# A mask by one product in place of two selects, and a new order of the opening stages, in a sliding-window attention and FFN kernel

## The chip, the cores and the metric

The kernel runs on one core of a Trainium2 chip. The metric is the device time of one execution in microseconds (us). The core has five engines with queues of their own: TensorE (PE; its weight loads are listed apart as PEld), VectorE (DVE), ScalarE (ACT), GpSimd (POOL) and SyncE (SP, which here only issues transfers). They run side by side, and wait for each other by semaphores. Within one queue the order written in the program holds: an instruction that waits holds back all behind it.

## The reference

Eight batches of eight heads with 576 positions of width 64 go through causal attention with a window of 64 positions. The heads are then laid side by side into 4608 tokens of width 512, which go through a multiplicative feed-forward network (FFN):

```python
scores = scale * np.matmul(q, k.transpose(0, 1, 3, 2))
rel = pos[:, None] - pos[None, :]
mask = (rel >= 0) & (rel < window)
attn = softmax(np.where(mask, scores, -1e9))      # over keys
x = np.matmul(attn, v)                            # then (batch*seq, heads*64)
a = x @ w1
b = x @ w2
h = a * b @ w3
out = h @ w_out
```

All inputs and the output are float32.

## The kernel before

**Attention.** The kernel works in float16 with float32 sums. For a batch, K and Q are loaded with the sequence folded onto 128 partitions, cast to float16 (`cast_qk`, L226; for batch 0 in thirds, `cast_third`, L229), transposed by PE into PSUM and copied out into `kT` and `qT` (`transposes`, L262 and L266). A batch is then six steps d: three segments of the sequence times two halves of the head pairs, so that batch 0 is d = 0 to 5 and batch 1 is d = 6 to 11. `scores(d)` multiplies K by Q into the PSUM tile `s_ps`, of which there is one; ACT takes the exponential into `pt` (L300), of which there are six; and POOL sets to zero what lies outside the window. It does so with pairs of `affine_select` (L308 and L310): one pair over 1024 elements a partition in the second and third segment, and two pairs, over 512 and 256, in the first. `values(d)` multiplies V, stored with columns of ones that give the sums, by `pt` into `o_ps` or `s_ps`; ACT makes the reciprocal of the sum by a logarithm and an exponential, and DVE writes the product into `xT`, a ring that holds four batches.

V of batch 0 is loaded in rows and brought into place by transposes (`transposes(0, "v", ...)`, then `keys_of_v`, L273 and L275). For later batches `load_v` (L241) writes V straight into `v16s`, with five DMAs issued by POOL, and `copy_v` (L245, L247) has DVE copy the halves of blocks that overlap.

**The fold.** As nothing is between w3 and w_out, the kernel computes their product once. `fold_t(fc)` transposes a block row of w3 (L492, L493), and `fold_mm(fc, half)` multiplies it by one half of w_out into `wc_sb` (L501, L503). w3 comes in four pieces (`load_w3(n)`, each for two fc), w_out in two halves.

**The FFN.** A group g is 512 tokens. `ffn_ab(g, fc)` for eight fc makes a and b on PE (L432), ACT copies a (L437), DVE multiplies (L438); `ffn_o(g, t)` for four t multiplies by the folded weights (L450), DVE copies (L452), and SP stores (`store`, L459).

**PSUM.** PE writes into tiles of four pools: `tp` (one), `s_ps` (one), `o_ps` (one) and `f_ps` (three). `three()` gives banks of the first three, in a stated order, to the three thirds of a transpose. `keep_busy(n)` issues n matmuls into `tp` whose result nobody reads.

**Order.** It is written out by hand: no scheduler moves anything. The order of calls in the program is the order on every queue. First come the loads of K and Q of batch 0 (SP and ACT queues) and a row of loads on POOL's queue, then the scores of batch 0 mixed with the fold, then the values of batch 0 with the rest of the fold, then FFN group 0 mixed with the scores and values of batch 1. Afterwards a loop goes through the FFN groups 1 to 8, and after each piece `tick(u)` adds the attention steps that are due by a count written in the code; that part isn't touched, apart from the mask inside `scores`. Loads of K and Q from batch 2 on go through SP and are held back by a small memset of the buffer that they write (`gate` in `load_qk`, L208); their casts are made by POOL.

Of the kernel before, what the change touches and what calls it, by code (L numbers as in the profile page):

```python
# [9 lines left out]
FP16 = mybir.dt.float16  # L10
I32 = mybir.dt.int32
ALU = mybir.AluOpType
# [3 lines left out]
P = 128  # L16
# [128 lines left out]
def kernel(  # L145
# [67 lines left out]
    def load_rows(b, which):  # L213

        t = sb.tile([P, 2, TI * D], FP16, name="rows", bufs=3)
        for hh in range(2):
            nc.gpsimd.dma_start(out=t[:, hh], in_=big_rows(which, b, hh))
        raws[which, b] = t
# [6 lines left out]
    def cast_qk(b, which, hh, cp):  # L225
        cp(t16_of(b, which)[:, :, hh * D:hh * D + D], raws[which, b][:, hh].rearrange("p (i d) -> p i d", d=D))  # L226
# [25 lines left out]
    def transposes(b, which, *cs, into=None, cps=None):  # L252

        t16 = t16s[which, b]
        if cs[0] == 0:
            turned[which, b] = sb.tile([P, NJ, S], FP16, name=which + "T", bufs=1 if which == "v" else 2)
        dst = turned[which, b]
        if into is None:
            into = [ps_t.tile([P, 6, P], FP16, name="tp")]
        for c, tp in zip(cs, into):  # L260
            for i in range(6):
                nc.tensor.transpose(tp[:, i, :], t16[:, 6 * c + i, :], ident16)  # L262
        if cps is None:
            cps = [dve_cp if which == "k" or c != 1 else act_cp for c in cs]
        for c, tp, cp in zip(cs, into, cps):
            cp(dst.rearrange("q j (p i) -> q j p i", i=TI)[:, :, :, 6 * c:6 * c + 6],  # L266
               tp.rearrange("q i (p j) -> q j p i", p=TP))

    def keys_of_v(b, js, into, cps):
# [4 lines left out]
        for j, tp, cp in zip(js, into, cps):  # L274
            cp(v16s[b % 2][:, :, j].rearrange("p c (a e) -> p c a e", a=2)[:, :, :, 0:D],  # L275
               tp.rearrange("p c (a e) -> p c a e", a=2))


    MASKS = [[(0, 1, 128, 0, 0), (128, 1, 64, 64, 0)]] + 2 * [[(0, 2, 128, 64, -64)]]
    probs, lns = {}, {}  # L280

    def scores(d):

        b, r = divmod(d, 6)
        si, jp = divmod(r, 2)
        kT, qT = turned["k", b], turned["q", b]
        seg = SEGS[si]
        w = sum(blk[2] for blk in seg)
        s_ps = ps_s.tile([P, 2, 2, 256], FP32, name="s_ps")
        for jj in range(2):  # L290
            j = 2 * jp + jj
            c0 = 0
            for (k0, q0, n, _) in seg:
                for a in range(2):
                    half = slice(a * D, a * D + D)
                    nc.tensor.matmul(s_ps[:, a, jj, c0:c0 + n], kT[half, j, k0:k0 + P], qT[half, j, q0:q0 + n],  # L296
                                     start=True, stop=True, skip_group_check=True)
                c0 += n
        pt = sb.tile([P, 2, 2, 256], FP16, name="pt", bufs=6)
        nc.scalar.activation(pt[:, :, :, 0:w], s_ps[:, :, :, 0:w], AF.Exp, bias=-SHIFT, scale=scale)  # L300

        rows = pt.rearrange("k a j n -> k (a j) n")
        for (lo, nb, n, off, step) in MASKS[si]:
            sl = rows[:, :, lo:lo + nb * n]
            pat = [[0, 4], [step, nb], [1, n]]
            if nb == 1:
                pat = [[0, 4], [1, n]]
            nc.gpsimd.affine_select(out=sl, in_=sl, pattern=pat, compare_op=ALU.is_ge,  # L308
                                    fill=0.0, base=off, channel_multiplier=-1)
            nc.gpsimd.affine_select(out=sl, in_=sl, pattern=[[-s, m] for s, m in pat], compare_op=ALU.is_ge,  # L310
                                    fill=0.0, base=63 - off, channel_multiplier=1)
        probs[d] = pt

    def values(d, pool=None):
# [154 lines left out]
    def load_w12(i, half):  # L469
        cols = slice(half * 512, half * 512 + 512)  # L470
        nc.gpsimd.dma_start(out=(w1_sb, w2_sb)[i][:, :, cols],
                            in_=(moe_w1, moe_w2)[i][:, cols].rearrange("(c p) n -> p c n", p=P))

    def load_wo(half):
        cols = slice(half * 256, half * 256 + 256)
        nc.gpsimd.dma_start(out=wo16[:, :, cols], in_=moe_w_out[:, cols].rearrange("(e p) m -> p e m", p=P))

    def load_w3(n):
        fc = 2 * n
        dst = w3a[:, 2 * fc:2 * fc + 4, :].rearrange("p (f a) n -> p f (a n)", f=2) if n < 2 else \  # L480
            xT[:, fc - 4:fc - 2, 2 * S:2 * S + DF]
        nc.gpsimd.dma_start(out=dst, in_=moe_w3[fc * P:fc * P + 2 * P].rearrange("(f p) n -> p f n", p=P))
# [12 lines left out]
    def fold_mm(fc, half, cp, nf=1):  # L495

        cols = slice(half * 256, half * 256 + 256)
        o_ps = ps_f.tile([P, 2, 256], FP32, name="f_ps")
        for f in range(nf):
            for ec in range(8):  # L500
                nc.tensor.matmul(o_ps[:, f], turned_w3(fc + f)[:, ec, :], wo16[:, ec, cols],  # L501
                                 start=(ec == 0), stop=(ec == 7), skip_group_check=True)
        cp(wc_sb[:, fc:fc + nf, cols], o_ps[:, 0:nf])  # L503
# [19 lines left out]
    def keep_busy(n):  # L523

        d = ps_t.tile([P, P], FP32, name="tp")
        for _ in range(n):
            nc.tensor.matmul(d, ident16, ident16, start=True, stop=True)
# [7 lines left out]
    def ones_of(i):  # L535
        nc.gpsimd.memset(v16s[i].rearrange("p c j (a e) -> p (c j a) e", a=2)[:, :, D:2 * D], 1.0)

    ones_of(0)
    load_w3(0)
    load_wo(0)  # L540
    load_rows(0, "v")
    for n in range(1, 4):
        load_w3(n)
    load_wo(1)
    ones_of(1)

    def bank(pool, name):

        t = pool.tile([P, 2, 1024] if name != "f_ps" else [P, 1, 1024], FP16, name=name)
        return t[:, 0, 0:768].rearrange("p (i n) -> p i n", i=6)  # L550

    def tp_bank():
        return ps_t.tile([P, 6, P], FP16, name="tp")

    def three():
        return [bank(ps_v, "o_ps"), tp_bank(), bank(ps_s, "s_ps")]

    keep_busy(75)
    for c in range(3):
# [11 lines left out]
    fold_t(1)  # L571
    for i in range(2):
        load_w12(i, 0)
    scores(2)
    fold_mm(0, 0, dve_cp)
    scores(3)
    load_rows(1, "k")
    fold_mm(1, 0, dve_cp)
    for hh in range(2):
        cast_qk(0, "v", hh, dve_cp)  # L580
    scores(4)
    keep_busy(10)
    transposes(0, "v", 0, 1, 2, into=[bank(ps_v, "o_ps"), tp_bank(), bank(ps_f, "f_ps")], cps=[dve_cp, act_cp, act_cp])
    fold_t(2)
    fold_t(3)
    scores(5)
    load_rows(1, "q")
    for i in range(2):
        load_w12(i, 1)
    load_v(1, 0, 2, 3)  # L590
    keys_of_v(0, [0, 1, 2], [bank(ps_v, "o_ps"), tp_bank(), bank(ps_f, "f_ps")], [act_cp, dve_cp, dve_cp])
    fold_mm(2, 0, act_cp)
    keys_of_v(0, [3], [tp_bank()], [dve_cp])
    fold_t(4)
    fold_mm(3, 0, act_cp)
    fold_t(5)
    values(0)
    fold_mm(4, 0, act_cp)
    fold_t(6)
    values(1, ps_s)  # L600
    fold_mm(5, 0, act_cp)
    fold_t(7)
    values(2)
    fold_mm(6, 0, dve_cp)
    values(3, ps_s)
    fold_mm(7, 0, dve_cp)
    values(4)
    fold_mm(0, 1, dve_cp, 2)
    values(5, ps_s)
    fold_mm(2, 1, dve_cp, 2)  # L610
    fold_mm(4, 1, dve_cp, 2)
    load_v(1, 4, 5)
    load_qk(2, "k", nc.gpsimd.memset)
    load_qk(2, "q")
    fold_mm(6, 1, dve_cp, 2)
    cast_qk(1, "k", 0, dve_cp)
    cast_qk(1, "k", 1, act_cp)
    for n in range(3):
        keep_sums(n)


    ffn_ab(0, 0)
    transposes(1, "k", 0, 1, 2, into=three(), cps=[dve_cp, act_cp, dve_cp])
    cast_qk(1, "q", 0, dve_cp)
    cast_qk(1, "q", 1, act_cp)
    for hh in range(2):
        cast_qk(2, "k", hh, pool_cp)
    ffn_ab(0, 1)
    transposes(1, "q", 0, 1, 2, into=three(), cps=[dve_cp, act_cp, dve_cp])
    ffn_ab(0, 2)  # L630
    scores(6)
    ffn_ab(0, 3)
    scores(7)
    copy_v(1, 1)
    for hh in range(2):
        cast_qk(2, "q", hh, pool_cp)
    ffn_ab(0, 4)
    scores(8)
    copy_v(1, 4)
    load_v(2, 0, 2, 3)  # L640
    ffn_ab(0, 5)
    scores(9)
    load_qk(3, "k")
    steps = [lambda fc=fc: ffn_ab(0, fc) for fc in range(6, 8)] + [lambda t=t: ffn_o(0, t) for t in range(4)]
    for d in range(6, 12):
        values(d, ps_s if d in (9, 11) else None)
        if d < 8:
            scores(d + 4)
        steps.pop(0)()
        store()  # L650
        if d == 6:
            load_v(2, 4, 5)
        if d > 8:
            transposes(2, "k", d - 9)
    for hh in range(2):
        cast_qk(3, "k", hh, pool_cp)
    transposes(2, "q", 0, 1, 2, into=three())
    load_qk(3, "q")
    copy_v(2, 1)
    copy_v(2, 4)  # L660
# [68 lines left out]
```

## Time and profile before

| | |
|---|---|
| median of 14 runs | 293.43 us (291.67 to 297.34) |
| profiled execution | 293.63 us |
| its span in the profile | 291.8 us |
| granted TensorE clock | 0.997 of full speed |
| PE busy | 275.7 us in 2429 matmuls |
| POOL busy | 180.0 us |
| POOL selects, L308 and L310 | 52.5 and 52.1 us, 64 of each |
| moved by DMA | 37.68 MB |

A line of the groups by shape reads: line, engine, operation, output and input, shapes, count; then busy time and the mean duration in ns; then the idle time of the engine just before these instructions and what ended it. In the list of waits each row has the waiting engine and line, what it waited for, the total in us, how many times, and the longest. In the table by stretch of time each engine has its busy time and its number of instructions. In the timeline and in the chain a row begins with the start in us and the duration.

### The profile page before, as it was taken

To read this page: it belongs to the slowest core of one execution; us is meant where nothing else is said; L and a number is where in the kernel's file an instruction comes from. 1 tells how busy PE (TensorE), PEld (TensorE's weight loads), DVE (VectorE), ACT (ScalarE), POOL (GpSimd) and SP (SyncE) were. 2 spreads that over 40 slices of the span, in tenths; PEclk is the share of its full clock that TensorE was granted. 3 is DMA by queue.
4 is the path that set the end of the run, shared out by engine and by line. 5 is a ranking of instruction groups with operands and counts; after the bars stand their busy time and mean duration, and the time that the engine had idled before them with its cause. 6 is when DMAs were issued, how large, how long until landed. Compare 5 with 4: busy or idle time off the path is not lost.

```text
span 291.8 us, 6248 instructions
## 1 busy us (share of the span) xinstructions
PE 275.7 (94%) x2429; PEld 161.9 (55%) x2429; DVE 184.4 (63%) x280; ACT 167.7 (57%) x277; POOL 180.0 (62%) x215
## 2 busy tenths in 40 slices
PE   7589998989899999999999999999999999999991
PEld 7568885445554555555555886455555545444441
DVE  0946558535868477778687866687767655464541
ACT  2565644674267646866777556478567765732300
POOL 8779933599479938695789473786595444402200
PEclk9999999999999999999999999999999999999998
DMA  6999999929797838294749550940193011002012
GB/s 243 247 210 204 209 211 372 169 16 93 149 388 107 80 124 317 14 105 140 299 31 125 187 211 0 193 37 2 37 172 22 2 73 73 2 36 110 2 61 89
DMA packets 48449, 37.68 MB, mean 129 GB/s; under 512 B 34160, under 2 KB 38512, under 8 KB 48416
## 3 DMA queue, kind: packets, MB, share of 16 engines
q0 software_dynamic: 38960, 11.14, 36.8%
q1 hardware_dynamic: 9024, 24.79, 23.2%
q10 hardware_dynamic: 432, 1.31, 1.3%
q8 instruction: 20, 0.33, 0.5%
q14 instruction: 13, 0.11, 0.1%
HBM read 38.80 MB, written 9.44 MB: 165 GB/s over the span
## 4 chain that ended last, share of the span: by engine, by line
PE 80%; POOL 7%; DVE 6%; ACT 2%; DMA 2%; issue 1%; DVEq 0%; POOLq 0%; SPq 0%; ACTq 0%
PE f_ps L432 38%; PE f_ps L450 20%; PE o_ps L354 5%; PE tp L262 5%; PE f_ps L501 5%; PE s_ps L296 4%; POOL pt L310 2%; POOL pt L308 2%; DMA stage<-in_k_dram 2%; DVE kT L266 1%; POOL v L241 1%; DVE k L229 1%; ACT pt L300 1%; PE f_ps L492 1%; PE s_ps L338 1%
## 5 line engine op out<-in xcount | busy, mean ns | idle before, releaser
L432 PE MATMUL f_ps<-xT,w_sb 128*128 128x512 f16 (+1 forms) x640 | 134.4, 358 | 0.0
L308 POOL TENSOR_SCALAR_AFFINE_SELECT pt<-pt 128x512 f16<-128x512 f16 (+1 forms) x64 | 52.5, 820 | 62.3 <-ACT pt L300 62.3
L432 PEld LDWEIGHTS <-w_sb 128*128 128x128 f16 x640 | 59.7, 98 | 50.3 <-issue 0.3
L450 PE MATMUL f_ps<-wc_sb,ab 128*128 128x512 f16 (+1 forms) x296 | 67.0, 373 | 0.1
L438 DVE TENSOR_TENSOR ab<-f_ps,a_sb 128x512 f16<-128x512 f32 x72 | 49.7, 691 | 22.1 <-PE f_ps L432 18.6
L300 ACT ACTIVATE pt<-s_ps 128x1024 f16<-128x1024 f32 (+1 forms) x48 | 45.7, 952 | 21.5 <-PE s_ps L296 19.1
L437 ACT COPY a_sb<-f_ps 128x512 f32<-128x512 f32 x72 | 41.7, 580 | 27.8 <-PE f_ps L432 26.8
L310 POOL TENSOR_SCALAR_AFFINE_SELECT pt<-pt 128x512 f16<-128x512 f16 (+1 forms) x64 | 52.1, 813 | 4.5
L363 DVE TENSOR_TENSOR xT<-o_ps,r 64x384 f16<-64x384 f32 x36 | 19.8, 549 | 38.7 <-ACT r L362 38.7
L450 PEld LDWEIGHTS <-ab 128*128 128x128 f16 x296 | 27.4, 98 | 27.9 <-issue 0.3
L360 ACT ACTIVATE ln_s<-o_ps 64x384 f32<-64x384 f32 x36 | 17.5, 487 | 32.6 <-PE o_ps L354 32.6
L452 DVE COPY t2k<-f_ps 128x512 f32<-128x512 f32 (+1 forms) x36 | 24.5, 682 | 11.8 <-PE f_ps L450 11.4
L241 POOL DMA_DIRECT2D v<-in_v_dram x35 | 29.7, 862 | 0.0
L354 PEld LDWEIGHTS <-v 128*128 128x128 f16 x288 | 18.1, 98 | 8.7 <-ACT pt L300 0.8
L296 PEld LDWEIGHTS <-kT 64*128 64x128 f16 x384 | 10.9, 94 | 18.6 <-issue 16.8
L354 PE MATMUL o_ps<-pt,v 128*128 128x128 f16 (+1 forms) x288 | 20.7, 215 | 0.4 <-DVE xT L364 0.4
L226 POOL CAST k<-stage 128x1152 f16<-128x1152 f32 x12 | 13.7, 1149 | 11.0 <-PE s_ps L262 8.1
L364 DVE TENSOR_TENSOR xT<-o_ps,r 64x384 f16<-64x384 f32 x36 | 20.2, 561 | 0.5
L296 PE MATMUL s_ps<-qT,kT 64*128 64x128 f16 (+1 forms) x384 | 18.2, 214 | 1.8 <-ACT pt L300 1.4
L362 ACT ACTIVATE r<-ln_s 128x384 f32<-128x384 f32 x36 | 18.8, 522 | 1.2
L361 ACT ACTIVATE ln_s<-o_ps 64x384 f32<-64x384 f32 x36 | 17.4, 482 | 0.4
L266 DVE COPY kT<-tp 128x768 f16<-128x768 f16 x18 | 17.1, 950 | 0.0
(88 smaller groups left out, 238.5 us busy)
## 6 DMA issues: line engine op xcount, KB each, us to landing
out_dram<-t2k SPq DMA_DIRECT2D x35, 256.0 KB
stage<-in_k_dram SPq DMA_DIRECT2D x13, 576.0 KB
stage<-in_q_dram SPq DMA_DIRECT2D x13, 576.0 KB
v<-in_v_dram POOLq DMA_DIRECT2D x28, 128.0 KB, 4.4
w_sb<-in_moe_w_dram POOLq DMA_DIRECT2D x4, 512.0 KB, 10.9
ab<-in_moe_w_dram POOLq DMA_DIRECT2D x2, 512.0 KB, 10.7
ab<-in_moe_w_out_dram POOLq DMA_DIRECT2D x2, 512.0 KB, 14.4
xT<-in_moe_w_dram POOLq DMA_DIRECT2D x2, 512.0 KB, 16.4
```

What stands on the lines that cost most here:

```text
L241: nc.gpsimd.dma_start(out=vh[lo:P, c], in_=v[b, :, s0:s0 + P - lo, :].rearrange("h s d -> s h d"))
L296: nc.tensor.matmul(s_ps[:, a, jj, c0:c0 + n], kT[half, j, k0:k0 + P], qT[half, j, q0:q0 + n], start=True, stop=True, skip_group_check=True)
L300: nc.scalar.activation(pt[:, :, :, 0:w], s_ps[:, :, :, 0:w], AF.Exp, bias=-SHIFT, scale=scale)
L308: nc.gpsimd.affine_select(out=sl, in_=sl, pattern=pat, compare_op=ALU.is_ge, fill=0.0, base=off, channel_multiplier=-1)
L310: nc.gpsimd.affine_select(out=sl, in_=sl, pattern=[[-s, m] for s, m in pat], compare_op=ALU.is_ge, fill=0.0, base=63 - off, channel_multip ...
L354: nc.tensor.matmul(o_ps[:, jj, o0:o0 + n], v16[:, si * 2 + bi, j0 + jj, a * D:a * D + P], pt[:, a, jj, c0:c0 + n], start=first, stop=(bi = ...
L364: nc.vector.tensor_tensor(xs[D:P], o_ps[D:P, :, 192:384], r[D:P], ALU.mult)
L432: nc.tensor.matmul(d[:, f * n + c0:f * n + c1], w[:, dc, (fc + f) * P:(fc + f + 1) * P], xT[:, dc, xc:xc + c1 - c0], start=first, stop=(dc ...
L437: act_cp(a_sb[:, 0:nf * n], a_ps[:, 0:nf * n])
L438: nc.vector.tensor_tensor(ab[:, fc:fc + nf, lo:hi], b_ps[:, 0:nf * n].rearrange("p (f n) -> p f n", f=nf), a_sb[:, 0:nf * n].rearrange("p ...
L450: nc.tensor.matmul(o_ps[:, 0:c1 - c0], ab[:, fc, t * P:t * P + P], wc_sb[:, fc, c0:c1], start=(fc == 0), stop=(fc == 7))
L452: cp(o_sb[:, c0:c1], o_ps[:, 0:c1 - c0])
```

## The change

The change has two parts.

The mask: `make_mask` builds once, on POOL, a float16 tile of 128 x 256 ones and zeros with a memset and two selects. In `scores`, POOL then multiplies `pt` by that tile, repeated over the four (half, pair) planes: one product of 1024 elements in the second and third segment, and two, of 512 and 256, in the first.

The order: the memset of ones for the second V buffer and the second piece of w3 stand ahead of the load of V of batch 0. Products of the fold come ahead of the next scores, and four of them instead of two ahead of V's transposes; ten filler matmuls become six there. K and Q of batch 1 are cast two steps sooner, and K is transposed before the first FFN piece. The gate of the loads of K of batch 2 is on DVE and behind the first FFN piece. The POOL casts of K and Q of batch 2, the copies of V of batch 1 and the values of batch 1 stand later among the FFN pieces. The banks of `three()` are in another order, and who copies them out is stated anew.

```diff
+    mask = const.tile([P, 2 * P], FP16)
+    def make_mask():
+        nc.gpsimd.memset(mask, 1.0)
+        pat = [[-64, 2], [1, P]]
+        nc.gpsimd.affine_select(out=mask, in_=mask, pattern=pat, compare_op=ALU.is_ge,
+                                fill=0.0, base=64, channel_multiplier=-1)
+        nc.gpsimd.affine_select(out=mask, in_=mask, pattern=[[-s, m] for s, m in pat], compare_op=ALU.is_ge,
+                                fill=0.0, base=63 - 64, channel_multiplier=1)
...
-        for (lo, nb, n, off, step) in MASKS[si]:
...
-            nc.gpsimd.affine_select(out=sl, in_=sl, pattern=pat, compare_op=ALU.is_ge,
-                                    fill=0.0, base=off, channel_multiplier=-1)
-            nc.gpsimd.affine_select(out=sl, in_=sl, pattern=[[-s, m] for s, m in pat], compare_op=ALU.is_ge,
-                                    fill=0.0, base=63 - off, channel_multiplier=1)
+        for (lo, n, m0) in [(0, 128, 128), (128, 64, 0)] if si == 0 else [(0, 256, 0)]:
+            sl = rows[:, :, lo:lo + n]
+            nc.gpsimd.tensor_tensor(sl, sl, mask[:, m0:m0 + n].unsqueeze(1).to_broadcast([P, 4, n]), ALU.mult)
...
     ones_of(0)
+    ones_of(1)
     load_w3(0)
     load_wo(0)
+    load_w3(1)
     load_rows(0, "v")
-    for n in range(1, 4):
+    for n in range(2, 4):
         load_w3(n)
     load_wo(1)
-    ones_of(1)
+    make_mask()
...
-        return [bank(ps_v, "o_ps"), tp_bank(), bank(ps_s, "s_ps")]
+        return [bank(ps_v, "o_ps"), bank(ps_s, "s_ps"), tp_bank()]
...
+    fold_mm(0, 0, dve_cp)
     scores(2)
-    fold_mm(0, 0, dve_cp)
+    fold_mm(1, 0, dve_cp)
     scores(3)
     load_rows(1, "k")
-    fold_mm(1, 0, dve_cp)
+    fold_t(2)
+    fold_t(3)
+    scores(4)
+    fold_mm(2, 0, act_cp)
     for hh in range(2):
         cast_qk(0, "v", hh, dve_cp)
-    scores(4)
-    keep_busy(10)
-    transposes(0, "v", 0, 1, 2, ...)
-    fold_t(2)
-    fold_t(3)
+    fold_mm(3, 0, act_cp)
     scores(5)
...
+    keep_busy(6)
+    transposes(0, "v", 0, 1, 2, ...)
+    fold_t(4)
+    fold_t(5)
     keys_of_v(0, [0, 1, 2], ...)
...
     values(5, ps_s)
-    fold_mm(2, 1, dve_cp, 2)
-    fold_mm(4, 1, dve_cp, 2)
-    load_v(1, 4, 5)
-    load_qk(2, "k", nc.gpsimd.memset)
-    load_qk(2, "q")
-    fold_mm(6, 1, dve_cp, 2)
     cast_qk(1, "k", 0, dve_cp)
     cast_qk(1, "k", 1, act_cp)
+    load_v(1, 4, 5)
+    fold_mm(6, 1, dve_cp, 2)
+    cast_qk(1, "q", 0, dve_cp)
+    cast_qk(1, "q", 1, act_cp)
...
+    transposes(1, "k", 0, 1, 2, into=three(), cps=[act_cp, dve_cp, dve_cp])
     ffn_ab(0, 0)
-    transposes(1, "k", 0, 1, 2, into=three(), cps=[dve_cp, act_cp, dve_cp])
-    cast_qk(1, "q", 0, dve_cp)
-    cast_qk(1, "q", 1, act_cp)
-    for hh in range(2):
-        cast_qk(2, "k", hh, pool_cp)
+    load_qk(2, "k", nc.vector.memset)
+    load_qk(2, "q")
     ffn_ab(0, 1)
-    transposes(1, "q", 0, 1, 2, into=three(), cps=[dve_cp, act_cp, dve_cp])
+    transposes(1, "q", 0, 1, 2, into=three(), cps=[act_cp, dve_cp, act_cp])
     ffn_ab(0, 2)
     scores(6)
     ffn_ab(0, 3)
     scores(7)
-    copy_v(1, 1)
+    for hh in range(2):
+        cast_qk(2, "k", hh, pool_cp)
+    ffn_ab(0, 4)
+    scores(8)
     for hh in range(2):
         cast_qk(2, "q", hh, pool_cp)
-    ffn_ab(0, 4)
-    scores(8)
-    copy_v(1, 4)
     load_v(2, 0, 2, 3)
-    ffn_ab(0, 5)
-    scores(9)
     load_qk(3, "k")
-    steps = [lambda fc=fc: ffn_ab(0, fc) for fc in range(6, 8)] + [lambda t=t: ffn_o(0, t) for t in range(4)]
+    steps = [lambda fc=fc: ffn_ab(0, fc) for fc in range(5, 8)] + [lambda t=t: ffn_o(0, t) for t in range(4)]
     for d in range(6, 12):
-        values(d, ps_s if d in (9, 11) else None)
-        if d < 8:
-            scores(d + 4)
         steps.pop(0)()
         store()
+        if d in (6, 8):
+            copy_v(1, {6: 1, 8: 4}[d])
+        if d < 9:
+            scores(d + 3)
+        values(d, ps_s if d in (9, 11) else None)
         if d == 6:
             load_v(2, 4, 5)
         if d > 8:
             transposes(2, "k", d - 9)
     for hh in range(2):
         cast_qk(3, "k", hh, pool_cp)
-    transposes(2, "q", 0, 1, 2, into=three())
+    steps.pop(0)()
+    store()
+    transposes(2, "q", 0, 1, 2, into=three(), cps=[act_cp, act_cp, dve_cp])
```

Where the diff has "...", lines that stay, or the like of which are shown, are left out: between the transposes of V and values(5), each fold piece of the second half of w3 stands one place sooner than before.

More of the change, by code (lines that the diff above doesn't have):

```diff
@@ L276, in keys_of_v @@
                tp.rearrange("p c (a e) -> p c a e", a=2))
-    MASKS = [[(0, 1, 128, 0, 0), (128, 1, 64, 64, 0)]] + 2 * [[(0, 2, 128, 64, -64)]]
     probs, lns = {}, {}
+    mask = const.tile([P, 2 * P], FP16)
[6 more added lines that the diff above has]
+                                fill=0.0, base=63 - 64, channel_multiplier=1)
     def scores(d):
@@ L302, in scores @@
         rows = pt.rearrange("k a j n -> k (a j) n")
-        for (lo, nb, n, off, step) in MASKS[si]:
[L304 to L308, printed above, removed]
-                                    fill=0.0, base=off, channel_multiplier=-1)
-            nc.gpsimd.affine_select(out=sl, in_=sl, pattern=[[-s, m] for s, m in pat], compare_op=ALU.is_ge,
-                                    fill=0.0, base=63 - off, channel_multiplier=1)
+        for (lo, n, m0) in [(0, 128, 128), (128, 64, 0)] if si == 0 else [(0, 256, 0)]:
+            sl = rows[:, :, lo:lo + n]
+            nc.gpsimd.tensor_tensor(sl, sl, mask[:, m0:m0 + n].unsqueeze(1).to_broadcast([P, 4, n]), ALU.mult)
         probs[d] = pt
@@ L573 @@
         load_w12(i, 0)
+    fold_mm(0, 0, dve_cp)
     scores(2)
-    fold_mm(0, 0, dve_cp)
+    fold_mm(1, 0, dve_cp)
     scores(3)
     load_rows(1, "k")
-    fold_mm(1, 0, dve_cp)
+    fold_t(2)
+    fold_t(3)
+    scores(4)
+    fold_mm(2, 0, act_cp)
     for hh in range(2):
         cast_qk(0, "v", hh, dve_cp)
-    scores(4)
-    keep_busy(10)
-    transposes(0, "v", 0, 1, 2, into=[bank(ps_v, "o_ps"), tp_bank(), bank(ps_f, "f_ps")], cps=[dve_cp, act_cp, act_cp])
-    fold_t(2)
-    fold_t(3)
+    fold_mm(3, 0, act_cp)
     scores(5)
@@ L590 @@
     load_v(1, 0, 2, 3)
+    keep_busy(6)
+    transposes(0, "v", 0, 1, 2, into=[bank(ps_v, "o_ps"), tp_bank(), bank(ps_f, "f_ps")], cps=[dve_cp, act_cp, act_cp])
+    fold_t(4)
+    fold_t(5)
     keys_of_v(0, [0, 1, 2], [bank(ps_v, "o_ps"), tp_bank(), bank(ps_f, "f_ps")], [act_cp, dve_cp, dve_cp])
-    fold_mm(2, 0, act_cp)
+    fold_mm(4, 0, act_cp)
     keys_of_v(0, [3], [tp_bank()], [dve_cp])
-    fold_t(4)
-    fold_mm(3, 0, act_cp)
-    fold_t(5)
+    fold_t(6)
+    fold_mm(5, 0, act_cp)
     values(0)
-    fold_mm(4, 0, act_cp)
-    fold_t(6)
+    fold_t(7)
+    fold_mm(6, 0, act_cp)
     values(1, ps_s)
-    fold_mm(5, 0, act_cp)
-    fold_t(7)
+    fold_mm(7, 0, act_cp)
     values(2)
-    fold_mm(6, 0, dve_cp)
+    fold_mm(0, 1, dve_cp, 2)
     values(3, ps_s)
-    fold_mm(7, 0, dve_cp)
+    fold_mm(2, 1, dve_cp, 2)
     values(4)
-    fold_mm(0, 1, dve_cp, 2)
+    fold_mm(4, 1, dve_cp, 2)
     values(5, ps_s)
-    fold_mm(2, 1, dve_cp, 2)
-    fold_mm(4, 1, dve_cp, 2)
-    load_v(1, 4, 5)
-    load_qk(2, "k", nc.gpsimd.memset)
-    load_qk(2, "q")
-    fold_mm(6, 1, dve_cp, 2)
     cast_qk(1, "k", 0, dve_cp)
     cast_qk(1, "k", 1, act_cp)
+    load_v(1, 4, 5)
+    fold_mm(6, 1, dve_cp, 2)
+    cast_qk(1, "q", 0, dve_cp)
+    cast_qk(1, "q", 1, act_cp)
     for n in range(3):
         keep_sums(n)
+    transposes(1, "k", 0, 1, 2, into=three(), cps=[act_cp, dve_cp, dve_cp])
     ffn_ab(0, 0)
-    transposes(1, "k", 0, 1, 2, into=three(), cps=[dve_cp, act_cp, dve_cp])
-    cast_qk(1, "q", 0, dve_cp)
-    cast_qk(1, "q", 1, act_cp)
-    for hh in range(2):
-        cast_qk(2, "k", hh, pool_cp)
+    load_qk(2, "k", nc.vector.memset)
+    load_qk(2, "q")
     ffn_ab(0, 1)
-    transposes(1, "q", 0, 1, 2, into=three(), cps=[dve_cp, act_cp, dve_cp])
+    transposes(1, "q", 0, 1, 2, into=three(), cps=[act_cp, dve_cp, act_cp])
     ffn_ab(0, 2)
```

## The prediction

> **What bounds the kernel now.** First the page's first part: TensorE is busy for 94% of the span, nothing else for more than 63%.
>
> ```profile
> PE 275.7 (94%) x2429; PEld 161.9 (55%) x2429; DVE 184.4 (63%) x280; ACT 167.7 (57%) x277; POOL 180.0 (62%) x215
> ```
>
> Next the table by stretch (length; busy time of PE, PEld, DVE, ACT, POOL; clock, DMA share, GB/s), cut where the stages change.
>
> ```profile
> 14.30:44.00 29.70, 27.81 (x397) 23.55 (x397) 16.32 (x27) 16.92 (x27) 22.43 (x30) 1.00 1.22 209
> 44.00:78.80 34.80, 31.33 (x315) 17.11 (x314) 21.68 (x32) 18.50 (x30) 23.37 (x27) 1.00 0.88 159
> 78.80:250.00 171.20, 170.82 (x1412) 94.83 (x1410) 120.84 (x188) 115.61 (x195) 116.11 (x138) 1.00 0.55 118
> ```
>
> From 78.8 to 250 us PE idles 0.4 us, so a cheaper mask gains nothing there. It idles 1.9 us in the fold stage and 3.5 us in the stage of batch 1; every reordering edit lies there or ahead. The waits of PE from 44 to 90 us name the second sum:
>
> ```profile
> PE o_ps L262 <- DVE q L226: 1.2, 1, 1.2
> PE s_ps L296 <- ACT pt L300: 1.1, 1, 1.1
> PE tp L262 <- DVE kT L266: 1.0, 1, 1.0
> PE o_ps L354 <- DVE xT L364: 0.4, 1, 0.4
> PE s_ps L338 <- POOL pt L310: 0.2, 1, 0.2
> ```
>
> In the fold stage the largest is 1.0 us, for the cast of V (L226). The chain that ended last nevertheless runs through POOL from 54 to 74 us:
>
> ```profile
> 63.08 2.60 POOL v L241 x3
> 65.68 1.13 POOL pt L308
> 74.06 0.64 PE s_ps L338 x16
> ```
>
> PE waits for it only 0.24 us: POOL and PE are tied there, and speeding up PE alone would turn into waits for POOL.
>
> [...]
>
> ```profile
> 7.27 3.13 DVE L229 CAST k<-stage 128x768 f16<-128x768 f32 x1
> 128.53 1.69 DVE L245 COPY v<-v 64x512 f16<-64x512 f16 x1
> ```
>
> The same cast took 0.59 just before, and the copy 0.29 where POOL was idle. The first got through when POOL's run of DMA issues ended at 10.0, the second between L308 and L310. So DVE gets in where POOL has a gap, and L310, waiting for L308, made one.
>
> [...] The groups by shape have:
>
> ```profile
> L308 POOL TENSOR_SCALAR_AFFINE_SELECT pt<-pt 128x1024 f16<-128x1024 f16 x32 | 35.6, 1112 | 34.5 <-ACT pt L300 34.5
> L310 POOL TENSOR_SCALAR_AFFINE_SELECT pt<-pt 128x1024 f16<-128x1024 f16 x32 | 35.2, 1099 | 2.3
> L513 POOL TENSOR_TENSOR chk<-lnsum 48x768 f32<-48x768 f32 x1 | 1.5, 1460 | 12.9 <-DMA out_dram<-t2k 12.9
> ```
>
> **Mask.** The selects took 0.42, 0.64 and 1.11 us for 256, 512 and 1024 elements: some 0.18 fixed. L513 then gives 1.28/768 = 1.67 ns an element, and the product over 1024 elements is 0.18 + 1.71 = 1.9 us against 2.21 + 0.07 gap; 512 + 256 cost 1.0 + 0.6 against 2.12 + 0.2. [...] Lower: a float16 product as fast as one select, 1.1. I take 1.9, since L513 is this operation, in another type. POOL saves 0.4 to 0.7 us a step, nearly all hidden. Building the mask (a memset and two selects of 256, about 1.2 us) fits ahead of the first exponential, which ends at 16.06.
>
> **Start, +0.4 us.** The q transposes fill o_ps, s_ps, tp rather than o_ps, tp, s_ps. The six filler matmuls behind them write tp, now emptied last (ACT, 14.82). Before, they ran from 14.31 under that copy; now their 0.34 us follow it, and scores(0) goes from 14.87 to about 15.25. The second memset of v (2.85) moves ahead of the weight loads: issues run from 6.9 to 13.1, not 4.0 to 10.0. K and Q fill the DMA engines until about 9.8, so the loads land little later. But the DVE casts of K, asked from 6.76, now meet a longer run of issues. In before, one got in at 6.9 next to an issue of V; V stands at 9.5 to 10.6 now. If the third cast gets in there it ends at 11.0 instead of 10.40, and Q's cast still ends at 13.4, because that was held by the memset until 12.98 and is now held by the last issue until 13.05. That is the value I take. Bounds: −1.0 if casts slip between issues; +2.7 if the third cast waits for 13.1.
>
> **Loads.** Landings in before: w3(0) 11.8, w_out 14.4, V 16.8 and 18.1, second w3 20.6, third 23.1: one after another, about 2.5 us for 512 KB. Swapped, the second w3 lands near 17.1 and V near 20.8. Needed: fold_t(2) at 20.0, V's casts at 21.9. Neither waits; cover 2.9 and 1.1 us.
>
> **Fold stage, −1.4 us.** Walking PE with row durations (scores 0.35, fold transposes 0.45, product 0.92, exponentials 0.81 and 1.02): fold_t(2), fold_t(3), fold_mm(2) and fold_mm(3) fill the place where PE waited 1.0 us for V's cast, and four fillers (0.2) go. Scores(3) and (4) wait 0.3 us each for the exponential before, as s_ps is single. The ACT copies of vT now stand behind exp(5), end at 26.6, and cost 0.5 us before keys_of_v. Values(0) comes at 30.25 with fold_t(7), fold_mm(6), (7) and half 1 left: 12.7 us, to 42.95, where ffn_ab(0,0) stood at 44.03. Net of the start, −1.4 (bounds −2.0 to −0.8).
>
> **Batch 1, −1.3 us.** Casts of K and Q two steps sooner: PE waits about 0.4 us for ACT's half of K (1.13, behind values(5)), but the 1.2 us for Q's cast goes. The bank order and ffn_o(0,3) placed before the q transposes remove the 1.0 us wait for tp; a full FFN step before scores(9) removes the 1.1. Scores(6) starts at 50.65 instead of 52.78.
>
> POOL now becomes the limit. From the mask of d=7 at 54.0 it has, without a pause: that mask 1.7, K cast 2.25, mask 1.9, Q cast 2.25, three V loads 2.6, mask 1.9, two V loads 1.6, masks 1.9 and 1.9, to 72.0. PE would stand for 2.4 us before values(9) and values(10). Also copy_v(1,1), moved behind ffn_ab(0,5), [...] its two copies get in about 58 to 60, so values(6) starts near 60.3 instead of 57.35; xT of values(6) and the next FFN product are queued on DVE behind them. That stall overlaps POOL's. Then ffn_ab(1,0) is at 76.9, against 78.84, start and fold included; with no copy stall 76.1. K of batch 2, gated now by a DVE memset at about 46.9 instead of POOL's at 38.95, lands about 52 and is cast at 55.7: hidden, cover 3.5 us. The later gate also leaves V of batch 1 the DMA engines: it landed at 54 to 57.5 before, and comes sooner. On SP, K and Q of batch 2 and K of batch 3 go out in one row ahead of the first store; each buffer is free, so nothing there waits. POOL's third to fifth V issue of batch 1 wait for landings of K and Q of batch 1 (about 35 to 37.5), with only the mask of d=6, at 52, behind them.
>
> **Sum.** +0.4 − 1.4 − 1.3 = −2.3 us. The profiled execution took 293.63 with span 291.8, so about 289.5 + 1.8 = 291.3; against the median 293.43, 291.1.
>
> **Rivals.** (1) *Faster still*: the product is nearer 1.1 us and casts slip between issues. POOL sheds 3 us, copies enter early, the start gains up to 1. All idle PE time is 5.4 us, so 287.9 to 289.9, say 289. [...]
> (2) *The start loses what is gained*: the K casts wait for the whole run of issues, as the 3.13 us row did. Scores(0) at about 17.2, 1.9 us later than in my sum: 293.0.
> (3) *Slower*: a single product leaves no L308–L310 gap. If copy_v is shut out through mask, Q cast and V loads, values(6) starts at 65.3. From there PE needs 16.3 us to ffn_ab(1,0): 81.6, or +2.8 us: 296.2. It decides when the second copy ends after 62.5. Against: copies at 55.8 to 58.2 got in within 0.1 us between small selects.
> (4) *The mask isn't cheaper*[...]
>
> **How the numbers follow.** Forecast 0.42 (own range 290.0 to 292.2); rivals 0.18, 0.20, 0.14, 0.06. The range 288.2 to 295.3 leaves out the deep end of (1) and most of (3). A measurement here tells about 0.5%, 1.5 us: faster 0.36 + 0.18 + 0.03 = 0.57; same 0.06 + 0.15 + 0.05 = 0.26; slower 0.17.
>
> **What would show it.** Scores(0) at 15.2 or 17; the product's mean[...]; no wait of PE for V's or Q's cast; the L245 and L247 copies near 58 to 60; values(9) or (10) waiting for POOL; ffn_ab(1,0) at about 77; then PE without idle time. A copy held past 62 us, or casts of K ending after 13, would make the prediction wrong.

## The result, and the profile after

The changed kernel takes 305.53 us (median of 10 runs, 303.58 to 307.35), against 293.16 for the kernel before in the same runs: a ratio of 1.042 [1.038, 1.045]. It is 4.2% slower, where 291.1 was predicted. The profiled execution's span is 304.8 us, 13.0 longer than the 291.8 before.

Page of the changed kernel: busy time of each engine, the granted clock in 40 slices.

```profile
PE 280.6 (92%) x2425; PEld 163.9 (54%) x2425; DVE 195.8 (64%) x277; ACT 170.3 (56%) x281; POOL 174.2 (57%) x153
...
PEclk9887799998999999999999999999999999999999
```

POOL has less to do than before (174.2 us against 180.0), as intended. But DVE is busy for 11.4 us longer with three instructions fewer, so some of its instructions became longer, and the clock is below full in the slices (7.6 us each) from 8 to 38 us and from 69 to 76. The groups by shape tell which instructions (busy time, mean in ns, then idle time before):

```profile
L312 POOL TENSOR_TENSOR pt<-pt,mask 128x1024 f16<-128x1024 f16 x32 | 68.1, 2132 | 39.3 <-ACT pt L307 39.3
...
L245 DVE COPY v<-v 64x512 f16<-64x512 f16 x14 | 18.4, 1314 | 1.1 <-DMA v<-in_v_dram 0.8
...
L226 DVE COPY k<-rows 128x1152 f16<-128x1152 f16 x3 | 9.4, 3156 | 0.0
L229 DVE CAST k<-stage 128x768 f16<-128x768 f32 x2 | 1.1, 580 | 6.8 <-DMA stage<-in_k_dram 6.8
```

Three of them in the kernel before:

```profile
L245 DVE COPY v<-v 64x512 f16<-64x512 f16 x14 | 8.7, 621 | 1.4 <-DMA v<-in_v_dram 1.1
...
L229 DVE CAST k<-stage 128x768 f16<-128x768 f32 x2 | 3.6, 1858 | 6.8 <-DMA stage<-in_k_dram 6.8
...
L226 DVE COPY k<-rows 128x1152 f16<-128x1152 f16 x3 | 2.2, 772 | 0.0
```

The product of 1024 takes 2.13 us, about as long as the pair of selects that it replaces (2.21 plus a gap of 0.07); those of 512 and 256 take 1.15 and 0.67. The copies from SBUF to SBUF on DVE changed most; those out of PSUM did not (`kT<-tp` of L266 has a mean of 950 ns before and after). L245 has a mean of 1314 ns where it had 621, and L226 (two casts of V and one of K) 3156 where it had 772; 447 ns is what an undisturbed L226 takes in this trace. L229, the cast of K at the start, went the other way, from 1858 to 580.

The waits of PE (total, times, longest, in us) show what these copies hold up. Before, the first of them was 1.0 us and the other three weren't in the list:

```profile
PE o_ps L262 <- DVE k L226: 6.7, 1, 6.7
...
PE o_ps L339 <- DVE v L247: 2.7, 1, 2.7
PE f_ps L433 <- DVE t2k L453: 2.3, 3, 1.0
PE f_ps L433 <- DVE ab L439: 2.1, 3, 1.4
```

The first is the wait for V of batch 0, in the fold stage. The timeline of that stage (start, duration, engine, line) shows both sides of it:

```profile
20.04 4.21 POOL L312 TENSOR_TENSOR pt<-pt,mask 128x1024 f16<-128x1024 f16 x2
21.39 8.94 DVE L226 COPY k<-rows 128x1152 f16<-128x1152 f16 x2
24.19 1.14 POOL L217 DMA_DIRECT2D rows<-in_k_dram  x2
25.34 4.20 POOL L312 TENSOR_TENSOR pt<-pt,mask 128x1024 f16<-128x1024 f16 x2
...
30.39 0.82 PE L262 MATMUL o_ps<-ident,k 128*128 128x128 f16 x6 [6.66 <-DVE k L226]
```

POOL runs from 20.04 without a pause: two products, two DMA issues, two products, two issues. The first cast of V starts at 21.39 and ends at 29.87, with the first of the last two issues; the second is over 0.47 later. So DVE did not wait for the product that was running alone, but through all four and the issues between them.

In the stage of batch 1 it is the second of the two copies of V that waits:

```profile
66.09 0.29 DVE L245 COPY v<-v 64x512 f16<-64x512 f16 x1
66.18 2.18 POOL L312 TENSOR_TENSOR pt<-pt,mask 128x1024 f16<-128x1024 f16 x1
66.41 2.09 DVE L247 COPY v<-v 64x512 f16<-64x512 f16 x1
68.56 0.64 PE L339 MATMUL o_ps<-pt,v 128*64 128x64 f16 x12 [2.73 <-DVE v L247]
69.13 3.03 PE L433 MATMUL f_ps<-xT,w_sb 128*128 128x512 f16 x8
```

L245 gets in behind POOL's casts of K, which ran from 63.98 to 66.2, and takes its bare 0.29; L247 is then held for the whole product. The last row shows a second cost: an FFN piece that took 1.90 us at full clock takes 3.03. The table by stretch (length; busy time of PE, PEld, DVE, ACT, POOL; clock, DMA share, GB/s) shows a low clock after both waits:

```profile
30.40:34.00 3.60, 3.60 (x35) 3.60 (x36) 1.57 (x2) 1.52 (x2) 2.59 (x4) 0.51 1.20 210
...
69.00:73.00 4.00, 4.00 (x39) 1.81 (x36) 1.25 (x2) 2.01 (x4) 4.00 (x5) 0.69 0.22 14
...
87.00:250.00 163.00, 158.49 (x1316) 88.09 (x1315) 123.04 (x175) 107.33 (x181) 105.20 (x88) 1.00 0.57 119
```

After the wait of 6.7 us the clock is half for 3.6 us, and PE does 1.8 us of work less in them; in the row behind the wait of 2.7 us it is half for about 2.5 us, 1.2 us of work less.

The last of those rows is the loop, where PE had idled 0.4 us in all from 78.8 on; now it idles 4.5 us from 87 to 250. One of its waits in the timeline:

```profile
135.60 1.16 POOL L226 CAST k<-stage 128x1152 f16<-128x1152 f32 x1
136.50 3.59 DVE L245 COPY v<-v 64x512 f16<-64x512 f16 x1
136.71 2.13 POOL L312 TENSOR_TENSOR pt<-pt,mask 128x1024 f16<-128x1024 f16 x1
138.79 1.15 POOL L226 CAST k<-stage 128x1152 f16<-128x1152 f32 x1
...
141.06 2.12 POOL L312 TENSOR_TENSOR pt<-pt,mask 128x1024 f16<-128x1024 f16 x1 [1.13 <-ACT pt L307]
...
141.88 1.45 DVE L245 COPY v<-v 64x512 f16<-64x512 f16 x1
...
144.42 1.02 PE L433 MATMUL f_ps<-xT,w_sb 128*128 128x512 f16 x4 [0.96 <-DVE t2k L453]
```

The first copy waits through a cast, a product and another cast, the next through the rest of a product. The output copies (L453) in DVE's queue behind them are late, the three tiles of f_ps stay full, and PE stands at 143.5. The loop has several such places.

Added up: scores(0) starts at 13.49 instead of 14.87, a gain of 1.4 us. The first piece of FFN group 1 starts at 86.81 instead of 78.84, a loss of 8.0. In between stand the two waits of 9.4 us and the 3.0 us of work lost to the clock behind them; that these 12.4 exceed the 8.0 leaves 4.4 us that the new order gains there, the start's 1.4 among them. (A third stretch at half clock, from 13.4 to 16.8 us, lies in between too, so this gain is after what that cost.) The rest of the span, +5.0 us, is the loop and what follows it.

### The profile page after: what moved, and what is told of

It reads as the page before. It is cut to its first block, busy times and chain, and to the rows that moved or that the text cites. A ratio compares the mean times of both kernels' runs of the same rounds, so it can differ in the third digit from the quotient of the medians.

```text
span 304.8 us, 6174 instructions
## 1 busy us (share of the span) xinstructions
PE 280.6 (92%) x2425; PEld 163.9 (54%) x2425; DVE 195.8 (64%) x277; ACT 170.3 (56%) x281; POOL 174.2 (57%) x153
## 4 chain that ended last, share of the span: by engine, by line
PE 73%; DVE 11%; issue 8%; ACT 5%; POOL 1%; DVEq 0%; POOLq 0%; ACTq 0%
PE f_ps L433 36%; PE f_ps L451 14%; PE tp L262 5%; PE o_ps L355 4%; PE s_ps L303 4%; PE f_ps L502 3%; DVE k L226 3%; PE tp L528 3%; DVE t2k L453 2%; PE f_ps L493 1%; DVE v L245 1%; DVE ab L439 1%; PE o_ps L339 1%; DVE v L247 1%; DVE xT L365 1%
## 5 line engine op out<-in xcount | busy, mean ns | idle before, releaser
L312 POOL TENSOR_TENSOR pt<-pt,mask 128x512 f16<-128x512 f16 (+1 forms) x64 | 96.6, 1522 | 90.0 <-ACT pt L307 90.0
L433 PE MATMUL f_ps<-xT,w_sb 128*128 128x512 f16 (+1 forms) x640 | 135.8, 360 | 4.4 <-DVE t2k L453 2.3
L453 DVE COPY t2k<-f_ps 128x512 f32<-128x512 f32 (+1 forms) x36 | 24.4, 681 | 11.1 <-PE f_ps L451 10.6
L245 DVE COPY v<-v 64x512 f16<-64x512 f16 x14 | 18.4, 1314 | 1.1 <-DMA v<-in_v_dram 0.8
L266 DVE COPY kT<-tp 128x768 f16<-128x768 f16 x19 | 18.0, 950 | 0.0
L226 POOL CAST k<-stage 128x1152 f16<-128x1152 f32 x12 | 13.7, 1150 | 3.2 <-issue 3.2
```

Of the source, the lines that this page charges most:

```text
L312: nc.gpsimd.tensor_tensor(sl, sl, mask[:, m0:m0 + n].unsqueeze(1).to_broadcast([P, 4, n]), ALU.mult)
L433: nc.tensor.matmul(d[:, f * n + c0:f * n + c1], w[:, dc, (fc + f) * P:(fc + f + 1) * P], xT[:, dc, xc:xc + c1 - c0], start=first, stop=(dc ...
L453: cp(o_sb[:, c0:c1], o_ps[:, 0:c1 - c0])
```

## The experiments

Four theories stand against each other. *No gap*: the single product leaves POOL's queue without a gap, and DVE's copies are shut out. *The order*: the new order costs the time, whatever the mask is made with. *Late V*: V of batch 0 lands later, since its load went behind a piece of w3. *A dear product*: what counts is POOL's own time for the mask. Unless said otherwise a diff is against the changed kernel. Where two kernels are compared, their ratios to the kernel before are subtracted and multiplied by 293 us.

### The new order with the old mask

```diff
-        for (lo, n, m0) in [(0, 128, 128), (128, 64, 0)] if si == 0 else [(0, 256, 0)]:
-            sl = rows[:, :, lo:lo + n]
-            nc.gpsimd.tensor_tensor(sl, sl, mask[:, m0:m0 + n]...)
+        for (lo, nb, n, off, step) in MASKS[si]:
...                                        # the pair of selects of the kernel before
-    make_mask()
```

> The new order kept whole, the mask made by the two selects again. Theory A (the single product leaves GpSimd without a gap, so that VectorE's copies from SBUF to SBUF[...], wait for the whole queue of GpSimd): each pair of selects has a gap, so the first cast of V takes under 3 us instead of 8.47, TensorE's 6.7 us wait for it and its half-speed clock behind it go, copies of V take under 1.8 us each, and the time is 288 to 293 us. Theory B (the new order itself costs the time, V's casts being asked for while GpSimd is busiest): the waits of 6.7 and 2.7 us stay and the time is above 299 us.

Measured: 292.0 us, ratio 0.993 [0.990, 0.996]. The order alone is a gain of 0.7%. The theory of the order falls, and the product costs 14 us here. The timeline shows the casts of V at the same place:

```profile
20.31 1.72 DVE L226 COPY k<-rows 128x1152 f16<-128x1152 f16 x2
20.47 1.24 POOL L316 TENSOR_SCALAR_AFFINE_SELECT pt<-pt 128x1024 f16<-128x1024 f16 x1
21.78 1.20 POOL L318 TENSOR_SCALAR_AFFINE_SELECT pt<-pt 128x1024 f16<-128x1024 f16 x1
```

Between 20.47 + 1.24 and 21.78 lies the gap in which L318 waits for L316. The casts are over at 22.03, where one product of 2.13 us in place of the pair, from 20.47 on, would have run to 22.6. A wait for L247 in batch 1 stays, and the clock is down after it (list of waits; table by stretch, whose next row, to 63, has 0.52):

```profile
PE o_ps L346 <- DVE v L247: 2.2, 1, 2.2
```

```profile
59.00:61.00 2.00, 2.00 (x17) 0.97 (x18) 0.49 (x1) 1.01 (x2) 2.00 (x3) 0.62 0.01 4
```

### The old order with the new mask

The kernel before with the product in the place of the selects, and make_mask behind the last memset of ones:

```diff
     ones_of(1)
+    make_mask()
```

> The old order kept, with only the mask made by one product. Theory A: the casts of V, asked for at 20.6 us, and the copies of V in every later batch wait for one or more products; the time is 297 to 304 us. Theory B: 291 to 295 us, since in the old order nothing urgent meets GpSimd's queue.

Measured: 307.78 us, ratio 1.048 [1.044, 1.052]. That is beyond the range expected, because a further place is hit, the second DVE cast of K at the start. PE waits 5.6 us for V's cast (L226) and 5.0 for that cast of K. The waits, then the timeline:

```profile
PE f_ps L262 <- DVE k L229: 5.0, 1, 5.0
```

```profile
6.71 6.62 DVE L229 CAST k<-stage 128x768 f16<-128x768 f32 x2 [6.71 <-DMA stage<-in_k_dram]
...
9.92 2.74 POOL L539 MEMSET v<- 128x3072 f16 x1
...
12.99 0.60 POOL L285 TENSOR_SCALAR_AFFINE_SELECT mask<-mask 128x256 f16<-128x256 f16 x1
```

The second of these casts waits through POOL's row of issues and both memsets, to 13.3. POOL's first pause there is the one in which L285 waits for the memset of the mask; L285 itself takes 0.60 where its twin takes 0.40. In the kernel before, the same cast got in at 10.0, between the last issue and the memset of V, although POOL made no pause there. The mask alone costs 14 us in this order too, so it isn't the mixture of the two parts that is slow.

### V's casts of batch 0 on ACT

```diff
     for hh in range(2):
-        cast_qk(0, "v", hh, dve_cp)
+        cast_qk(0, "v", hh, act_cp)
```

> The changed kernel with the two casts of V of batch 0 on ScalarE (about 1.15 us each)[...]. Theory A: the wait of 6.7 us shrinks to under 1.5 us and the clock stays at full speed from 24 to 34 us; what the copies of V cost later stays: 296 to 299 us. Theory C (V itself lands late because the second piece of w3 goes first): TensorE still waits about 6 us for the casts and the time stays at 303 to 307 us.

Measured: 299.63 us, ratio 1.0205 [1.016, 1.025]; 2.1%, 6.2 us, comes back, and the time is 0.6 us above the range expected. ACT casts in 1.15 us, when it is asked, from the same loads, and PE waits 0.9 us for it:

```profile
L226 ACT COPY k<-rows 128x1152 f16<-128x1152 f16 x3 | 3.3, 1147 | 0.0
```

So V was not late, and that theory falls. The wait of 2.7 us for L247 and those of 2.4 and 2.1 us at f_ps are left.

### All these copies on ACT

V's casts as above, and copy_v:

```diff
-        dve_cp(vh[0:D, c], vh[D:P, c - 1])
+        act_cp(vh[0:D, c], vh[D:P, c - 1])
         if c == 1:
-            dve_cp(vh[D:P, 1], vh[0:D, 2])
+            act_cp(vh[D:P, 1], vh[0:D, 2])
```

> The changed kernel, product on GpSimd, with the casts of V of batch 0 and all of copy_v on ScalarE. Theory A says that nothing else is lost to the product: with no VectorE copy from SBUF to SBUF left after the opening but the two of K and Q of batch 1, TensorE's waits for VectorE (4.4 us at f_ps, 2.7 us before values(6)) go and the time is 290 to 294 us. Theory D (the length of the product): 298 us or more.

Measured: 294.1 us, ratio 1.004 [1.002, 1.006]. With every product still on POOL, 3.75% or 11.0 of the lost 12.3 us come back; the copies are shown to carry most of the loss. Against the same order with selects (0.993) some 3.3 us remain. Selects with the copies on ACT were not run, so how much of that is the product's own length, and how much the copies' time on ACT, stays open. After the wait for the identity at the very start, which every kernel here has, the largest waits of PE are two for casts on ACT, 1.3 us together, and one for the mask. The groups by shape, then the waits:

```profile
L245 ACT COPY v<-v 64x512 f16<-64x512 f16 x14 | 8.6, 617 | 0.3
```

```profile
PE s_ps L339 <- POOL pt L312: 1.1, 1, 1.1
```

### A gap made on purpose

A second product, of one column of each plane, waits for the first; times 0 or 1 twice, nothing else changes:

```diff
             nc.gpsimd.tensor_tensor(sl, sl, mask[:, m0:m0 + n]...)
+            nc.gpsimd.tensor_tensor(sl[:, :, 0:1], sl[:, :, 0:1], mask[:, m0:m0 + 1]...)
```

> The changed kernel with, behind every product, a second product of one column a plane of the same tile (ones and zeros, so the values stay), which has to wait for the first: it makes GpSimd's work longer by some 0.3 us an instruction and opens a gap. Theory A: the first cast of V takes under 3.5 us, copies of V under 2.6 us, and the time falls to 291 to 298 us, although GpSimd works longer. Theory D (what counts is how long the product holds GpSimd, 2.13 us): the waits stay or grow, 305 us or more.

Measured: 300.68 us, ratio 1.025 [1.021, 1.028]: above the range expected, but 1.7%, 5.0 us, faster than the changed kernel, although POOL has 64 instructions and 13.8 us more to do. In the fold stage the gap did its work:

```profile
20.50 3.58 DVE L226 COPY k<-rows 128x1152 f16<-128x1152 f16 x2
21.23 2.14 POOL L312 TENSOR_TENSOR pt<-pt,mask 128x1024 f16<-128x1024 f16 x1
23.46 0.31 POOL L313 TENSOR_TENSOR pt<-pt,mask 128x4 f16<-128x4 f16 x1
```

Both casts take 3.58 us instead of 8.94, and end within 0.7 us of the gap at 23.37. The miss lies elsewhere: the gap comes once in 2.1 us rather than once in 1.1, L247 has a mean of 943 ns, and PE still waits 3.4 us for it and 5.1 us at f_ps. The gap let these casts in; it didn't make the product equal to two selects.

### The product on DVE

```diff
-            nc.gpsimd.tensor_tensor(sl, sl, mask[:, m0:m0 + n]...)
+            nc.vector.tensor_tensor(sl, sl, mask[:, m0:m0 + n]...)
```

> The changed kernel with the product made by VectorE. Theory A: GpSimd's queue is then short, so casts and copies no longer wait for masks[...]: 289 to 296 us. Theory E (VectorE becomes the limit[...]): 297 us or more.

Measured: 295.44 us, ratio 1.009 [1.006, 1.012]. The casts of V are back at 453 ns, and the product of 1024 takes 0.745 us there in the mean. L247 has a mean of 709 ns (303 in the kernel before), and PE waits 1.4 us for it. And 37 us more work in DVE's queue stand ahead of its copies out of PSUM: PE waits 1.6 and 1.2 us at f_ps.

### The product in the loop alone

Selects for batches 0 and 1, product from batch 2 on, in the new order (the diff is against that order with selects; make_mask is called again):

```diff
-        for (lo, nb, n, off, step) in MASKS[si]:
+        for (lo, nb, n, off, step) in MASKS[si] if b < 2 else []:
...
+        for (lo, n, m0) in [] if b < 2 else [(0, 128, 128), (128, 64, 0)] if si == 0 else [(0, 256, 0)]:
```

> The new order with selects in batches 0 and 1 and the product from batch 2 on. Theory A: in the loop copy_v of V waits behind casts and a product (3.6 us each time in the changed kernel), the copies of the FFN result queue behind it, and TensorE waits 4.4 us in all for PSUM: 295.5 to 298 us, against 292.0 for selects throughout. If the loop hides all that: 291.5 to 293 us.

Measured: 297.55 us, ratio 1.013 [1.009, 1.017], against 0.993 for the new order with selects throughout: 2.0%, 5.9 us, are lost from batch 2 on, near the 5.0 us by which the changed kernel's span grew there. The waits of the loop are those of the changed kernel, 2.3 us for the output copies and 1.8 for the products of a and b.

### What the new order is worth

With selects, four variants ask where the order's gain goes. The first puts copy_v(1, 1) back behind scores(7):

```diff
     scores(7)
+    copy_v(1, 1)
...
-        if d in (6, 8):
-            copy_v(1, {6: 1, 8: 4}[d])
+        if d == 8:
+            copy_v(1, 4)
```

> The new order with selects, and copy_v(1, 1) back between scores(7) and the casts of K of batch 2. Theory A: VectorE then asks while GpSimd has only small selects in its queue, so the 2.2 us wait of TensorE before values(6) goes, and with it the half-speed clock that followed it in the run with selects (a 1.73 us FFN piece took 3.4 us): 287 to 289.5 us, 0.977 to 0.987 of before. If the clock has another cause, only 2.2 us go or less: 289.5 to 291 us.

Measured: 292.59 us, ratio 0.9985 [0.9965, 1.0005]: no gain beside the 0.993 without it, a miss. The copies now take 0.29 and 0.39 us at 53.0, and the wait for them is gone, but PE meets another at once:

```profile
PE s_ps L346 <- POOL pt L318: 2.6, 1, 2.6
```

The mask of d = 9 stands on POOL behind the casts of Q of batch 2 and three V issues (60.1 to 64.9). So POOL's order has to go with it (the diff is against the kernel with the early copy):

```diff
-    for hh in range(2):
-        cast_qk(2, "q", hh, pool_cp)
-    load_v(2, 0, 2, 3)
...
         if d == 6:
-            load_v(2, 4, 5)
+            for hh in range(2):
+                cast_qk(2, "q", hh, pool_cp)
...
+    load_v(2, 0, 2, 3)
+    load_v(2, 4, 5)
     for hh in range(2):
         cast_qk(3, "k", hh, pool_cp)
```

> Selects, the new order, the early copy_v(1, 1), and on GpSimd's queue the masks of d = 9 to 11 ahead of work that isn't due: the casts of Q of batch 2 behind the mask of d = 9, the five V loads of batch 2 behind that of d = 11. If GpSimd's queue in batch 1 is what held the run with the early copy (TensorE waited 2.6 us for the mask of d = 9), that wait goes and the time is 287.5 to 290 us, 0.980 to 0.989 of before. If the late V loads hold copy_v of batch 2 instead, VectorE stalls near 77 us and the time stays at 291 to 293 us.

Measured: 289.68 us, ratio 0.987 [0.983, 0.990], the lowest time here, 0.6% under the new order with selects. Its span is 287.4 us, its clock 0.999, and after the start its largest wait of PE is short; the one for POOL's mask is down to 0.6 us:

```profile
PE tp L262 <- DVE kT L266: 1.0, 1, 1.0
```

The other two put the bank order of the q transposes of batch 0 back to o_ps, tp, s_ps, once in the new order with selects and once in the kernel just shown:

> The new order with selects, the q transposes of batch 0 again into o_ps, tp, s_ps. The filler matmuls then run under the copy of qT: the 0.9 us wait of TensorE for tp goes and scores(0) starts 0.3 to 0.4 us sooner, so the time falls by about 0.4 us against the run with selects, 291 to 292 us; if the fillers weren't on the path, no change.

> The same with the old bank order in the q transposes of batch 0: 0.1 to 0.5 us less than the kernel without it.

Measured: ratios 0.996 [0.994, 0.9985] and 0.987 [0.984, 0.990], beside 0.993 and 0.987 without it. The wait at tp falls from 0.9 to 0.7 us, and nothing of it is left in the time.

## Why the prediction was wrong

**The failed step is "Fold stage, −1.4 us".** It walks PE with row durations and puts the wait for V's casts, asked for at 21.9, at nothing. A reading against that stood higher up, on the K cast and on L245: DVE gets in where POOL has a gap, and L310, waiting for L308, made one (the L245 shown there was over at 130.22, 0.15 us after POOL's pause began). It was applied to the casts at the start and to copy_v of batch 1, not to V's casts. When these were asked for, at 21.4, POOL had masks and issues in one row, and the first cast took 8.47 us. PE's wait of 6.7 us and the half clock behind it cost 8.5 us. The fold's last product ended at 51.19 us instead of 44.30: with the start's gain of 1.4 taken out, a loss of 8.3 in this stage (the half clock from 13.4 to 16.8 us is in it), where a gain of 1.4 was forecast. With the casts on ACT 6.2 us of the time came back.

**"A cheaper mask gains nothing there" (78.8 to 250 us)** fits what was measured, but the sum then took the loop as unchanged. The step looked at PE's idle time, which tells what a saving is worth, not what a longer wait of DVE costs. There are 21 copies of V for the batches from 1 on; L245's mean rose by 0.69 us, and the loop lost 5.0 us, or 5.9 with the product there alone. The sum has no term for this.

**Start, +0.4** had the wrong sign: −1.4. The K casts took 0.58 us each between the issues; the bound of −1.0 was the nearer one. What it feared, a cast held to the end of POOL's run, did occur, in the old order with the new mask (5.0 us at PE). The prediction read the K cast of the kernel before as let in where the run of issues ended; but a memset stood right behind that run (it starts at 9.94), so that was no gap. Why the casts got in early in the new order was not tested.

**Batch 1, −1.3.** The two copies of V were said to take about 2 us longer; L247 took 2.09, and PE waited 2.7. The size was right, but the clock after it, 1.2 us, was left out. The prediction's own end point for this stage, 76.9 instead of 78.84, makes 1.9 us in all and so 0.9 for this stage, not 1.3; beside the loss that is small. The wait of PE for POOL's mask that it feared isn't in the changed kernel's list. That POOL and PE are tied there shows with selects: with the copy early, PE waited 2.6 us for POOL's mask, and with POOL's order changed too the whole order brings 1.3%.

**Mask.** 1.9 us was taken from L513; measured 2.13 (1.15 and 0.67 for 512 and 256), 0.2 more. By the difference between 512 and 1024 elements the product costs 1.91 ns an element, and POOL saves almost nothing on a step of 1024. **Loads**: no wait of PE for a load is in the list, as said.

**The rivals.** The third named the mechanism, that a single product leaves no gap between L308 and L310, but for one place, copy_v of batch 1, and at +2.8 us. That place cost 3.9 us with its clock in the profiled execution; V's casts, more than twice as much, and the loop were not in it. Its argument against, that copies got in "between small selects", spoke of the gaps that the change removes. The first rival fell with the product at 2.13 us, where it had 1.1. The fourth, a mask that isn't cheaper, came near for POOL itself, with 2.13 us for 2.28; 11.0 of the 12.3 us lost came back with the copies on ACT. The price named by the second was paid only in the old order.

## What to carry to other kernels

The product had two prices here: its length, 2.13 us for 2.28, and the gap that it took away. Before two short dependent instructions become one long one, list the SBUF-to-SBUF copies of VectorE that are asked while GpSimd's queue is full, walk each of them to the next pause of that queue, where at the latest it got in here (over within 0.42 us of the pause's start), and see what is queued behind it on VectorE; here ScalarE made the same copies in 0.62 and 1.15 us in the mean, with every product still on GpSimd. And a reordering needs the queue of every engine that it touches: moving one copy forward gained nothing, and only with GpSimd's order changed as well did the new order's gain grow from 0.7% to 1.3%.

## What the runs showed of the hardware

**A held copy can wait through several GpSimd instructions, not one.** Beside a busy POOL some copies of DVE from SBUF to SBUF took many times their bare duration: in the changed kernel a cast of V 8.47 us, across four products and the two DMA issues between them, and a copy of V 3.59 us, across three instructions; in the old order with the new mask a cast of K 6.07 us, across issues and memsets. Their bare durations are 0.45, 0.29 and 0.58.

Where a held copy gets in is shown in part. In the traces of the kernel before and of the changed kernel, each of the 13 copies that were still held at a pause of POOL of 0.07 us or more, such as the one before an instruction that waits for its predecessor, was over within 0.42 us of the pause's start; the cast of K just named was over 0.41 us after POOL's pause at 12.92. At a seam without a pause the outcome varied. L247 in batch 1 got in after one product, at 68.36, with a cast right behind, and was over at 68.50; the first cast of V got in behind the fourth product, which ended at 29.55, with an issue right behind; and of two K casts at the same seam, at 10.0, the one of the kernel before got in and was over at 10.40, and the one of the old order with the new mask didn't, and was over at 13.33. What decides at such a seam stays open.

**A wait of PE can cost more than itself.** Behind the wait of 6.7 us the clock was 0.51 for 3.6 us. Behind shorter waits it varied: it was 0.50 from 69 to 71 us behind the one of 2.7 us in the changed kernel, and 0.52 from 61 to 63 behind the one of 2.2 us in the new order with selects, but 1.00 behind one of 2.7 us at the same place with V's casts alone on ACT, and 1.00 from 64 to 84 around and behind one of 2.6 us with the early copy. The rows with V's casts alone on ACT:

```profile
54.00:64.00 10.00, 7.26 (x80) 3.54 (x79) 5.15 (x7) 5.55 (x9) 9.67 (x10) 1.00 0.46 185
64.00:74.00 10.00, 7.97 (x86) 4.10 (x86) 8.34 (x7) 5.96 (x11) 9.56 (x7) 1.00 0.97 73
```

The wait of 2.7 us is what PE lacks in the first row. So the length of the wait alone doesn't tell. Executions of one kernel differ too: with the copies on ACT, those at a mean clock of 1.000 took 293.35 to 294.12 us, those at 0.986 to 0.989 took 294.76 to 295.76. In the profiled execution of the changed kernel the clock also stood at 0.50 from about 13.4 to 16.8 us, where PE had waited at most 0.9 us, and in that of the kernel with V's casts alone on ACT, which is the same up to there, it was 1.00 from 13 to 17; what set it off stays open.
